# Second chunk's tokens loaded ahead of the third query weights, and the layer-norm statistics of two token tiles moved in the opening of an attention and SwiGLU block

## Chip, cores, metric

One core of one Trainium2 chip (trn2). The metric is the device time of one execution in microseconds (us), lower is better. The kernel before takes 1170.86 us (median of 3 runs, 1169.75 to 1174.22).

A ratio is always the mean time of one kernel's fast runs over the mean of the other's of the same rounds, so it is not quite the ratio of the medians that stand beside it.

## The reference, cut to what matters

```python
def reference(A_x, A_k_cache, A_v_cache, A_wq, A_wo, B_x, B_w_gate, B_w_up, B_w_down, c, w_mod):
    # x: 1 x 2048 x 1024, bf16; 32 query heads of 128, 4 key/value heads, the last 512 keys
    sa, ca, ga, sb, cb, gb = (silu(c) @ w_mod) in six pieces
    h = layernorm(x) * (1 + ca) + sa
    x = x + ga * attention(h, A_k_cache, A_v_cache, A_wq, A_wo)   # q = h @ wq, softmax, @ v, @ wo
    h = layernorm(x) * (1 + cb) + sb
    return x + gb * swiglu(h, B_w_gate, B_w_up, B_w_down)
```

The tokens are worked in four chunks of 512, each of four tiles of 128 tokens. This case is about the first 50 us: chunk 0 (tiles 0 to 3) is normalised and its first query heads are projected, attention over chunk 0 begins, and meanwhile chunk 1 (tiles 4 to 7) has to be loaded, get its mean and reciprocal deviation, be normalised and be transposed by DMA.

## The kernel before

The kernel is written for raw engines. A small tracker (`T.op`) puts each operation into its engine's queue in program order and adds the waits that its buffers need. On VectorE an operation that waits held those behind it: in the changed kernel below, tile 4's normalisation waited 1.21 us for its reciprocal deviation, until 32.65 us, and tile 5's statistics, whose tokens had landed at 28.57, started after it, at 33.11.

The loads, all in the queue of SyncE:

```python
            # ... loads of chunk 0, modulation weights, query weights 0 and 1, k(0)
            for k2 in range(DT // 2):
                load_wsa(k2)
            load_v(0)
            load_k(1)
            load_wq(2)        # query weights of heads 8 to 11, 1 MB
            load_x(1)         # tokens of chunk 1 (tiles 4 to 7), 1 MB
            for gk in range(2, Hkv):
                load_k(gk)
            # ...
```

Statistics, normalisation and transposition of a tile of chunk 1 (`stats` is BN_STATS on half a tile, `aggr` combines the halves on VectorE and makes the reciprocal deviation on GpSimd):

```python
            def ln_stats(t):
                stats(t, t % 2, 0)
                yield
                stats(t, t % 2, 1)
                aggr(t % 8, t % 2)
                yield

            def norm_turn(ch, tt):
                t = ch * TPC + tt
                norm(t, t % 8, t % 2, half=True)                   # VectorE
                T.op(Q_ln[t % 2], lambda: SP.dma_start_transpose(hT[ch % 2][:, :, tt * P:(tt + 1) * P], nscf[t % 2]),
                     reads=[B_ns4[t % 2]], writes=B_hT[ch % 2])
```

The end of the opening:

```python
            q_bias_mm(0, 2, BB)
            q_shifted(0)
            qproj_mm(7, QB0[7], HK, DT)
            q_raw(7)                    # evacuates head 7's bank, on ScalarE
            q_shifted(1)
            for dt in range(DT):
                shift(dt)               # 8 operations on VectorE
            stats_now(TPC)              # tile 4, VectorE
            stats_now(TPC + 1)          # tile 5, VectorE
```

And what each iteration of the attention loop does first. Iteration 1 emits the first scores and the bias matmuls of heads 2 and 3, whose results VectorE copies out of bank `QB` (the "bq copy"); iteration 2 projects head 8 into the same bank, so that projection waits for the bq copy:

```python
            def pre0(i):
                if 2 <= i < NQ0:
                    q_shifted(i)
                # ... the k transposes of iterations 2, 3, 4 and their evacuation on VectorE
                if i == 1:
                    scores(0)
                if i in (1, 3, 5):
                    q_bias_mm(i + 1, i + 3, QB)                    # ends with the bq copy on VectorE
                if i < NQ0 + 1:
                    if i % 2 == 0:
                        qproj(NQ0 - 1 + i // 2)                    # i = 2: head 8, into bank QB
                elif i + 3 < NDI:
                    qproj(i + 3)
                if i < 5:
                    norm_turn(1, i - 1)
                if 1 < i < 4:
                    stats_now(TPC + i)                             # tiles 6 and 7
                # ... modulation of chunk 1 at i = 7 and 8
            # then in the same iteration: scores(i - 1), pv(i - 2)
```

`scores(i)` are 4 matmuls and two exponentials on ScalarE; `pv(i)` multiplies the probabilities with v, and VectorE evicts the product with a reciprocal and a multiplication.

The softmax here doesn't subtract the row's maximum and nothing guards it: scores larger than these inputs give would overflow.

## Time and profile before

| | before |
|---|---|
| median, range (3 runs) | 1170.86 us, 1169.75 to 1174.22 |
| span of the profiled execution | 1168.8 us |
| TensorE busy | 1150.6 us (98%) |
| longest wait of TensorE | 4.18 us, at 31.3 us |

First the page's busy times, engine by engine (us, share of the span, instructions):

```profile
span 1168.8 us, 18210 instructions
PE 1150.6 (98%) x7087; PEld 585.7 (50%) x7087; DVE 819.9 (70%) x1641; ACT 527.6 (45%) x735; POOL 67.3 (6%) x135
```

TensorE has 18 us of idle time in all. Next, the waits of TensorE between 25 and 60 us (who waited for whom; us in total, times, longest):

```profile
PE ps L272 <- DVE bq L668: 4.2, 1, 4.2
PE ps L272 <- ACT arena L790: 0.2, 1, 0.2
PE ps L272 <- DVE arena L812: 0.2, 1, 0.2
```

The timeline shows what stands behind that one wait. Columns: start, duration, engine, line, operation, output and input, count, and in brackets the idle time before it and what ended it:

```profile
29.61 0.60 ACT L658 ACTIVATE arena<-ps 128x512 f32<-128x512 f32 x1 [4.46 <-PE ps L272]
29.89 2.19 DVE L678 TENSOR_SCALAR arena<-arena,mod_bf 128x512 f16<-128x512 f16 x8
30.91 0.38 PE L276 MATMUL ps<-arena 128*128 128x128 bf16 x4
32.10 1.42 DVE L413 BATCH_NORM_STATS2 st<-x_res 128x6 f32<-128x512 bf16 x2
33.56 0.21 DVE L417 BATCH_NORM_AGGREGATE mv<-st 128x2 f32<-128x12 f32 x1
33.69 1.37 DVE L413 BATCH_NORM_STATS2 st<-x_res 128x6 f32<-128x512 bf16 x2
35.09 0.21 DVE L417 BATCH_NORM_AGGREGATE mv<-st 128x2 f32<-128x12 f32 x1
35.22 0.10 DVE L668 COPY bq<-ps 128x2 f32<-128x2 f32 x1
35.47 5.34 PE L272 MATMUL ps<-arena 128*128 128x512 f16 x28 [4.18 <-DVE bq L668]
...
36.57 0.15 PEld L272 LDWEIGHTS ps<-arena 128*128 128x128 bf16 x1 [0.28 <-issue]
36.99 0.15 PEld L272 LDWEIGHTS ps<-arena 128*128 128x128 bf16 x1 [0.28 <-issue]
...
38.94 0.69 DVE L647 CAST arena<-ps 128x512 bf16<-128x512 f32 x1 [2.44 <-PE ps L272]
...
41.74 0.69 DVE L812 TENSOR_TENSOR arena<-ps,rl 128x512 f16<-128x512 f32 x1
42.49 0.68 PE L272 MATMUL ps<-arena 128*128 128x129 bf16 x9 [0.18 <-DVE arena L812]
```

Read it from the top. TensorE is done at 31.29 (30.91 + 0.38). VectorE does the 8 shifts, the statistics of tiles 4 and 5 (L413, L417) and only then the tiny bq copy (L668), which lets head 8's projection start at 35.47. Its weight loads are then 0.42 us apart, against 0.22 us at 22.5 to 24.6 us: the clock is at half rate (granted 0.50 from 35.65 to 39.06 us). VectorE in its turn waits 2.44 us for that slow projection (L647). The last two lines are the first PV eviction and the second PV product, which waits for it. **The start of the second PV product, 42.49 us here, is the point by which I compare all kernels below.**

The chain of waits, followed back from the end of the program, tells the same stretch differently:

```profile
19.50 12.58 DMA x_res<-in_A_x_dram
32.10 0.71 DVE st L413
```

It says that the statistics waited for the landing of chunk 1's tokens, 12.58 us after their issue. But the shifts (29.89 + 2.19) also end at 32.08. The two tie, and the chain names one of them.

### The profile page before, as it was taken

Reading aid. Unit: us, or ns where it says so; the run is one execution under the profiler, and the core shown is the slowest. Engines: PE = TensorE matmul, PEld = TensorE weight load, DVE = VectorE, ACT = ScalarE, POOL = GpSimd, SP = SyncE. Lnnn points to the kernel's source line nnn. Section 1 sums busy time; section 2 is a strip of 40 time slices with the busy share of each in tenths; the row PEclk is TensorE's granted clock in tenths of the full one; section 3 lists DMA queues with packets and bytes.
Section 4 is the critical chain, followed back from the end, with each engine's and each line's share of the span. In section 5 each row is a group of like instructions: output and inputs, shape, how many; then the busy total and the mean of one; then the engine's idle time right before and its main releaser. Section 6 shows DMA issues by size and latency. Waiting matters only on the chain.

```text
span 1168.8 us, 18210 instructions
## 1 busy us (share of the span) xinstructions
PE 1150.6 (98%) x7087; PEld 585.7 (50%) x7087; DVE 819.9 (70%) x1641; ACT 527.6 (45%) x735; POOL 67.3 (6%) x135
## 2 busy tenths in 40 slices
PE   9899999999999999999999999999999999999998
PEld 5465555654445666665444444444444444444443
DVE  4867897748476777777566798767558777776535
ACT  3666777740117777787110345454110444445010
POOL 1100131000000111111000010000000000000000
PEclk9999999999999999999999999999999999999999
DMA  9679899787816888844776232333775424234343
GB/s 325 135 194 213 200 225 211 178 179 203 256 36 161 192 203 187 210 106 107 192 182 187 73 108 73 97 84 99 207 182 156 122 73 109 73 100 133 125 156 108
DMA packets 289765, 179.98 MB, mean 154 GB/s; under 512 B 130448, under 2 KB 277904, under 8 KB 289680
## 3 DMA queue, kind: packets, MB, share of 16 engines
q1 hardware_dynamic: 226736, 92.31, 36.3%
q10 hardware_dynamic: 54304, 55.05, 14.9%
q0 software_dynamic: 8640, 31.46, 9.2%
q8 instruction: 56, 0.92, 0.4%
q14 instruction: 29, 0.24, 0.1%
HBM read 128.45 MB, written 19.92 MB: 127 GB/s over the span
## 4 chain that ended last, share of the span: by engine, by line
PE 90%; DMA 4%; DVE 3%; SPq 2%; issue 1%; ACT 1%; POOL 0%; ACTq 0%; DVEq 0%; POOLq 0%
PE ps L272 90%; DMA arena<-arena 1%; DMA x_res<-in_A_x_dram 1%; DMA wo_sum<-arena 1%; DMA arena<-in_A_wo_dram 1%; DVE arena L820 1%; DVE st L413 1%; DVE arena L891 0%; SPq L382 0%; SPq L341 0%; ACT arena L790 0%; DVE arena L812 0%; SPq L364 0%; SPq L355 0%; ACT nsc L823 0%
## 5 line engine op out<-in xcount | busy, mean ns | idle before, releaser
L272 PE MATMUL ps<-arena 128*128 128x512 f16 (+2 forms) x6782 | 1143.9, 331 | 14.6 <-DVE bq L668 4.2
L272 PEld LDWEIGHTS ps<-arena 128*128 128x128 bf16 (+1 forms) x6782 | 575.6, 98 | 574.9 <-issue 10.0
L790 ACT ACTIVATE arena<-ps 128x1024 bf16<-128x1024 f32 x256 | 261.3, 1022 | 54.8 <-PE ps L272 42.9
L823 ACT ACTIVATE tmp<-ps 128x512 f32<-128x512 f32 x166 | 99.1, 597 | 302.3 <-PE ps L272 289.6
L891 DVE TENSOR_TENSOR arena<-arena 128x512 f16<-128x512 bf16 x328 | 133.1, 418 | 3.1
L820 DVE TENSOR_TENSOR arena<-ps,tmp 128x512 bf16<-128x512 f32 (+1 forms) x134 | 91.8, 685 | 46.1 <-PE ps L272 34.4
L812 DVE TENSOR_TENSOR arena<-ps,rl 128x512 f16<-128x512 f32 x128 | 88.5, 691 | 6.5 <-DMA arena<-arena 2.1
L823 ACT ACTIVATE nsc<-ps 128x512 f32<-128x512 f32 x84 | 50.1, 596 | 93.2 <-PE ps L272 90.9
L820 DVE TENSOR_TENSOR arena<-ps,nsc 128x512 f16<-128x512 f32 x84 | 57.3, 686 | 40.3 <-PE ps L272 31.1
L809 DVE RECIPROCAL rl<-ps 128x4 f32<-128x4 f32 x128 | 23.0, 180 | 87.9 <-PE ps L272 86.8
L1029 DVE TENSOR_TENSOR arena<-arena 128x2048 f16<-128x2048 f16 (+3 forms) x56 | 56.0, 1010 | 13.5 <-PE ps L272 12.9
L1502 ACT ACTIVATE arena<-arena 128x512 f16<-128x512 f16 x84 | 49.9, 624 | 30.7 <-DVE arena L820 30.7
L820 DVE TENSOR_TENSOR tmp<-ps,tmp 128x512 f32<-128x512 f32 x32 | 22.1, 689 | 55.7 <-ACT tmp L823 47.6
L823 ACT ACTIVATE arena<-ps 128x512 f32<-128x512 f32 x16 | 9.6, 598 | 91.9 <-PE ps L272 91.9
L941 DVE TENSOR_TENSOR arena<-arena 128x512 f16<-128x512 bf16 x120 | 47.8, 419 | 2.8 <-DMA arena<-in_A_wo_dram 1.7
L413 DVE BATCH_NORM_STATS2 st<-x_res 128x6 f32<-128x512 bf16 x62 | 42.3, 682 | 4.1 <-DMA x_res<-in_A_x_dram 3.7
L1517 DVE TENSOR_TENSOR arena<-arena 128x512 f16<-128x512 f16 x84 | 34.9, 415 | 0.2
L1097 DVE TENSOR_TENSOR tmp<-tmp,rowb 128x512 f32<-128x512 f32 x48 | 33.2, 692 | 1.6
L427 DVE TENSOR_SCALAR nsc<-x_res,mv,rstd 128x1024 f16<-128x1024 bf16 (+1 forms) x30 | 16.1, 538 | 25.6 <-DMA arena<-nsc 25.6
L594 DVE SCALAR_TENSOR_TENSOR arena<-arena 128x1024 bf16<-128x1024 bf16 x24 | 29.2, 1215 | 0.0
L1098 DVE TENSOR_TENSOR arena<-tmp,x_res 128x512 bf16<-128x512 f32 x32 | 22.1, 692 | 1.1
L820 DVE TENSOR_TENSOR arena<-ps,rowb 128x512 f16<-128x512 f32 x28 | 19.3, 689 | 3.9 <-ACT rowb L823 3.9
(81 smaller groups left out, 326.9 us busy)
## 6 DMA issues: line engine op xcount, KB each, us to landing
arena<-in_A_wq_dram SPq DMA_DIRECT2D x28, 512.0 KB, 5.0
arena<-wo_sum ACTq DMA_DIRECT2D x7, 2048.0 KB, 9.1
arena<-in_B_w_gate_dram SPq DMA_DIRECT2D x28, 512.0 KB, 4.0
arena<-in_B_w_up_dram SPq DMA_DIRECT2D x28, 512.0 KB, 5.0
arena<-wd_sum ACTq DMA_DIRECT2D x8, 1792.0 KB, 8.0
arena<-in_B_w_down_dram ACTq DMA_DIRECT2D x6, 1792.0 KB, 7.3
arena<-in_A_wo_dram POOLq DMA_DIRECT2D x16, 512.0 KB, 5.1
wo_sum<-arena POOLq DMA_DIRECT2D x16, 512.0 KB, 4.9
```

What stands on the lines that cost most here:

```text
L272: T.op(PE, lambda: TE.matmul(out_ap, lhsT, rhs, start=start, stop=stop, skip_group_check=skip), reads=reads, writes=[bank_buf])
L413: T.op(DVE, lambda: V.bn_stats(st_[sl][:, hf * 6:hf * 6 + 6], x_res[:, t, hf * 512:hf * 512 + 512]), reads=[B_x[t]], writes=[B_st[sl]])
L790: T.op(ACT, lambda: A.activation(ex_s[es][:, 2 * kp:2 * kp + 2, :], banks2(SCB + 2 * kp), AF.Exp, scale=att_scale), writes=[PB[SCB + 2 * k ...
L812: T.op(DVE, lambda: V.tensor_tensor(o_s[os_].rearrange("p (a b) d -> p a b d", a=2), psap(PVB * 512, [[512, 2], [130, 2], [1, P]]), rlb, A ...
L820: T.op(DVE, lambda: V.tensor_tensor(out, bank(ba), other, ADD), reads=[ob2], writes=[PB[ba], ob])
L823: T.op(ACT, lambda: A.activation(dst, bank(bk), AF.Copy), writes=[PB[bk], db])
L891: T.op(st, lambda: eng.tensor_tensor(o, a, b, op), reads=rd, writes=[wr])
L941: T.op(DVE, lambda: V.tensor_tensor(o, a, b, SUB), reads=rd, writes=[wr])
L1029: T.op(DVE, lambda: V.tensor_tensor(o, a, b, SUB), reads=rd, writes=[sb])
L1097: T.op(DVE, lambda: V.tensor_tensor(tm, tm, rw, MULT), reads=[B_row[row]], writes=[tb])
L1502: T.op(ACT, lambda: A.activation(o, s_, AF.Silu), reads=[sb], writes=[ob])
L1517: T.op(DVE, lambda: V.tensor_tensor(gu[blk][:, p, :], o, s_, MULT), reads=[sb, ob], writes=[B_gu[blk][p]])
```

## The change

The intent: let the tokens land before the weights; compute the first of the four tiles' statistics on ScalarE, which is idle there, by two passes with an accumulator (sum, then sum of squared differences); and move tile 5's behind the bq copy, into iteration 1, so that tiles 5, 6 and 7 come one per iteration (6 and 7 stay where they were).

```diff
             load_v(0)
             load_k(1)
+            load_x(1)
             load_wq(2)
-            load_x(1)
@@
+            def stats_act(t):
+                sl = t % 8
+                o, ob = nsc4[t % 2], B_ns4[t % 2]
+                T.op(ACT, lambda: A.activation(o, x_res[:, t, :], AF.Copy, accum_out=acc[:, 0:1]), reads=[B_x[t]], writes=[ob, B_acc])
+                T.op(POOL, lambda: g.tensor_scalar(mv[sl][:, 0:1], acc[:, 0:1], 1.0 / D, None, op0=ALU.mult),
+                     reads=[B_acc], writes=[B_mv[sl]])
+                T.op(ACT, lambda: A.activation(o, x_res[:, t, :], AF.Square, bias=mv[sl][:, 0:1], scale=-1.0, accum_out=acc[:, 1:2]),
+                     reads=[B_x[t], B_mv[sl]], writes=[ob, B_acc])
+                rstd_of(sl, acc[:, 1:2], B_acc, 1.0 / D)
@@
             qproj_mm(7, QB0[7], HK, DT)
+            stats_act(TPC)
             q_raw(7)
             q_shifted(1)
             for dt in range(DT):
                 shift(dt)
-            stats_now(TPC)
-            stats_now(TPC + 1)
@@
-                if 1 < i < 4:
+                if 1 <= i < 4:
                     stats_now(TPC + i)
```

## The prediction

> **What bounds the kernel.** The page: TensorE is busy 1150.6 of 1168.8 us (98%), so at most 18 us can be won without removing matmuls. The longest wait of TensorE is 4.2 us on the bias copy (DVE bq), in the opening. The timeline shows it: TensorE ends the first scores and the k transpose at 31.29 us and starts the ninth query projection (head 8) at 35.47. That projection reuses the bank which the bq copy on VectorE frees, and VectorE, in order, first does 8 shifts (29.89 to 32.08) and the statistics of tiles 4 and 5 (32.10 to 35.3). Chunk 1's tokens land at 32.08 (issue 19.50 + 12.58 in the chain), just as the shifts end; wq part 2 lands near 29.2 (issue 18.83 + 10.4). After the gap the projection's 8 matmuls take 3.45 us (0.43 each; 1.89 us for 8 at 22.6): TensorE has gone cold. [...]
>
> **What the change does.**
> 1. Tokens and wq part 2 swap landings (1 MB each, 2.9 us apart): tokens ~29.2, weights ~32.1.
> 2. Tile 4's statistics leave VectorE (two BN_STATS and the aggregate, 1.6 us) for ScalarE, idle between 25.2 and 29.6. Costed with the opening's own such pass (copy 1.06, square 1.15, reads, POOL; 3.7 us end to end): 29.2 to ~32.0 on ScalarE, rstd ready ~33.0.
> 3. Tile 5's statistics move behind the bq copy and tile 4's normalisation.
> New costs: the evacuation of head 7 moves from 29.6 to ~32.0, the first exponentials from 30.28 to ~32.6 (done ~34.8 instead of 32.4).
>
> **On the critical path.** VectorE: shifts end 32.08, bq copy ~32.2, so TensorE starts head 8 at ~32.3 (weights 32.1) instead of 35.47; gap ~1 us, no cold clock, projection ~1.8 instead of 3.45 us. That would be nearly 5 us, but VectorE becomes the limit: it waits for rstd of tile 4 to ~33.0, normalises (0.45), does tile 5's statistics (1.6), shift, k copy, head 8's copy (from ~35.8; before 38.94), normalise 5, statistics 6, then the first PV product's eviction at ~38.6 (before 41.74) . TensorE waits at the second PV (~39.3; before 42.49), of the order of 1 us. VectorE's own sum: 1.6 us of statistics gone, 2.4 us of waiting for the cold projection gone, 0.9 us of new waiting: **3.1 us**. By 47 us everything is about 3.1 us earlier; from there TensorE is saturated, loads are issued from program order and shift along, and I expect the gain kept to the end.
>
> **Predicted: 1170.86 - 3.1 = 1167.8 us, range 1165.3 to 1170.3.** Chances: faster by over 2% 0.01, within 2% 0.98, slower 0.01.
>
> **What would show it.** TensorE's wait on bq of 4.2 us gone, replaced by ~1 us at 31.3 and by 1 to 2 us in waits on ScalarE's exponentials and VectorE's PV eviction before 45 us; head 8's matmuls 0.22 us each; tokens landing ~29.2 and weights ~32.1; ScalarE's two statistics passes 29.2 to 32; the 128x4 reciprocals of the first PV at ~38.5 instead of 41.6; TensorE busy ~1.6 us less in total.
>
> **What would make it wrong.** If loads don't complete in issue order, tokens land later and ScalarE, stuck in order, holds head 7's evacuation and the exponentials: the gain shrinks by the delay. If weights land after ~34, TensorE waits there again. If a later limit that doesn't shift (background weight sums through memory, 159 to 181 us in the chain) takes the 3 us back, the total is unchanged.

## The result

| | before | after |
|---|---|---|
| first comparison, 4 runs each | 1170.88 us (1169.75 to 1174.22) | 1166.36 us (1165.51 to 1167.93) |
| ratio after / before | | 0.9958, 95% interval 0.9935 to 0.9981 |
| span of the profiled execution | 1168.8 us | 1164.3 us |
| all later control runs | 1169.86 us median of 42 | 1166.43 us median of 16 (with the 4 above) |

So the change is 0.3 to 0.4% faster: 4.5 us in the first four runs, 3.4 us over all runs.

The page and the waits of TensorE between 25 and 60 us, after:

```profile
span 1164.3 us, 18217 instructions
PE 1148.6 (99%) x7087; PEld 585.3 (50%) x7087; DVE 818.1 (70%) x1638; ACT 529.4 (45%) x739; POOL 68.9 (6%) x136
```

```profile
PE ps L272 <- DVE arena L821: 1.4, 1, 1.4
PE ps L272 <- DMA arena<-in_A_wq_dram: 1.0, 1, 1.0
PE ps L272 <- ACT arena L799: 0.5, 2, 0.3
```

The wait on the bq copy is gone. In its place are 1.0 us for the weights, 0.5 us for exponentials and 1.4 us for the first PV eviction (L821 is L812 of before). The timeline of the same stretch:

```profile
28.59 1.06 ACT L730 ACTIVATE nsc<-x_res 128x1024 bf16<-128x1024 bf16 x1 [4.14 <-DMA x_res<-in_A_x_dram]
29.19 2.19 DVE L678 TENSOR_SCALAR arena<-arena,mod_bf 128x512 f16<-128x512 f16 x8
30.21 0.38 PE L276 MATMUL ps<-arena 128*128 128x128 bf16 x4
30.39 1.15 ACT L733 ACTIVATE nsc<-x_res,mv 128x1024 bf16<-128x1024 bf16 x1 [0.65 <-POOL mv L731]
31.29 0.15 DVE L668 COPY bq<-ps 128x2 f32<-128x2 f32 x1
31.54 0.58 ACT L658 ACTIVATE arena<-ps 128x512 f32<-128x512 f32 x1
31.62 2.33 PE L272 MATMUL ps<-arena 128*128 128x512 f16 x10 [1.02 <-DMA arena<-in_A_wq_dram]
32.02 4.16 ACT L799 ACTIVATE arena<-ps 128x1024 bf16<-128x1024 f32 x4
32.65 0.55 DVE L427 TENSOR_SCALAR nsc<-x_res,mv,rstd 128x1024 f16<-128x1024 bf16 x1 [1.21 <-POOL rstd L527]
33.11 1.42 DVE L413 BATCH_NORM_STATS2 st<-x_res 128x6 f32<-128x512 bf16 x2
...
35.37 0.68 DVE L647 CAST arena<-ps 128x512 bf16<-128x512 f32 x1
...
38.16 0.69 DVE L821 TENSOR_TENSOR arena<-ps,rl 128x512 f16<-128x512 f32 x1
...
38.91 1.08 PE L272 MATMUL ps<-arena 128*128 128x129 bf16 x16 [1.36 <-DVE arena L821]
```

The tokens land at 28.57 and ScalarE takes tile 4 (L730, L733); the bq copy follows the shifts at once (31.29); head 8 starts when the weights land (31.57); VectorE waits 1.21 us for tile 4's reciprocal deviation and is then the busy engine up to the first PV eviction. The second PV product starts at 38.91.

Lining up the two traces matmul by matmul (both have 7087, in the same order) gives the lead of the changed kernel over the course of the program:

```
where                                   start before   lead of after
200th matmul, before anything changed     24.49          0.70 us
head 8, first matmul                      35.47          3.86
head 8, last matmul                       38.27          5.14
second PV product                         42.49          3.59
up to 70 us                                              3.59
after the waits at 104 to 119 us         118.8           3.85
after a wait at 183 us                   184.0           4.51
end                                                      4.54
```

Of the 4.54 us, 0.70 were there before the change could act, 2.89 came between the opening and the second PV product, and 0.95 came from later waits. By the last matmul of head 8 the change had won 4.44 us (5.14 - 0.70), and 1.55 of them were given back before the second PV product.

### The profile page after: what moved, and what is told of

The parts are those of the page before. It is cut to its first block, busy times and chain, and to the rows that moved or that the text cites. A ratio compares the mean times of both kernels' runs of the same rounds, so it can differ in the third digit from the quotient of the medians.

```text
span 1164.3 us, 18217 instructions
## 1 busy us (share of the span) xinstructions
PE 1148.6 (99%) x7087; PEld 585.3 (50%) x7087; DVE 818.1 (70%) x1638; ACT 529.4 (45%) x739; POOL 68.9 (6%) x136
## 4 chain that ended last, share of the span: by engine, by line
PE 91%; DVE 3%; DMA 3%; SPq 1%; ACT 1%; issue 1%; POOL 0%; DVEq 0%; ACTq 0%; POOLq 0%
PE ps L272 91%; DMA arena<-arena 1%; DMA x_res<-in_A_x_dram 1%; DVE arena L829 1%; DMA arena<-in_A_wo_dram 1%; DVE st L413 1%; SPq L382 0%; DVE arena L900 0%; DMA wo_sum<-arena 0%; SPq L341 0%; ACT arena L799 0%; SPq L364 0%; DVE arena L821 0%; ACT nsc L832 0%; SPq L310 0%
## 5 line engine op out<-in xcount | busy, mean ns | idle before, releaser
L821 DVE TENSOR_TENSOR arena<-ps,rl 128x512 f16<-128x512 f32 x128 | 88.5, 691 | 6.0 <-DMA arena<-arena 1.6
```

The costliest lines, as they stand in the source:

```text
L821: T.op(DVE, lambda: V.tensor_tensor(o_s[os_].rearrange("p (a b) d -> p a b d", a=2), psap(PVB * 512, [[512, 2], [130, 2], [1, P]]), rlb, A ...
```

## Experiments

Theory: (1) VectorE's order of work, not the landing of the tokens, held TensorE; (2) behind that, VectorE's chain from the shifts to the first PV eviction is the limit, so what counts is when that chain starts and how much stands in it; (3) the clock at half rate is part of the cost of the gap. The main rivals: the tokens' landing was the limit (the chain of waits), or all that counts is TensorE's own wait.

For each run I give the time and, from its one profile, the lead of the second PV product over the before profile, with the lead at 24.5 us (most of it comes from the clock at the very start, see the end of "The clock alone") taken off. I call it the net lead.

| run | median us (runs) | ratio to before, 95% interval | net lead at the second PV |
|---|---|---|---|
| the change, first comparison | 1166.36 (4) | 0.9958, 0.9935 to 0.9981 | 3.59 - 0.70 = 2.89 |
| e0_change_again | 1166.52 (6) | 0.9965, 0.9945 to 0.9985 | 3.23 - 0.36 = 2.87 |
| e10_change_control | 1166.79 (6) | 0.9972, 0.9958 to 0.9987 | 3.02 - 0.54 = 2.48 |
| e1_loads_only | 1171.55 (6) | 1.0007, 0.9992 to 1.0021 | -0.07 - 0.40 = -0.47 |
| e2_old_loads | 1168.70 (6) | 0.9991, 0.9978 to 1.0004 | 0.15 - 0.16 = -0.01 |
| e3_order_only | 1168.68 (6) | 0.9986, 0.9973 to 0.9999 | 0.42 - 0.23 = 0.19 |
| e4_warm | 1167.32 (6) | 0.9976, 0.9964 to 0.9988 | 1.56 - 0.57 = 0.99 |
| e5_tile4_dve | 1169.15 (6) | 0.9991, 0.9968 to 1.0013 | 2.05 - 0.60 = 1.45 |
| e6_tokens_earlier | 1165.04 (6) | 0.9953, 0.9936 to 0.9971 | 3.27 + 0.09 = 3.36 |
| e7_stats_later | 1166.76 (6) | 0.9967, 0.9949 to 0.9985 | 3.37 + 0.51 = 3.88 |
| e8_combined | 1167.24 (5) | 0.9967, 0.9953 to 0.9981 | 4.85 + 0.04 = 4.89 |
| e9_order_warm | 1168.98 (5) | 0.9988, 0.9972 to 1.0004 | 1.19 - 0.27 = 0.92 |
| e11_tokens_earlier_warm | 1165.03 (5) | 0.9969, 0.9955 to 0.9982 | 3.91 - 0.52 = 3.39 |

All gave the right result. The intervals of the ratios reach 1.4 to 2.7 us to each side, so the times alone separate only the larger differences; the net lead separates finer ones, but it is one execution each.

### The loads alone

```diff
+            load_x(1)
             load_wq(2)
-            load_x(1)
```

> The kernel before with only the two loads swapped. My theory (VectorE's program order is what held TensorE: shifts end at 32.08 us and the statistics of tiles 4 and 5 stand ahead of the bias copy): tokens land near 28.6 to 29.2, but VectorE still reaches the statistics only at about 32.1, so TensorE's wait on the bias copy stays 3.9 to 4.3 us and the total within 0.5 us of before. Rival (the profile's chain names the landing of the tokens, 12.6 us, so their landing was the limit): VectorE's statistics start up to 3 us earlier, the wait shrinks to about 1 us, and the total falls by about 3 us.

Measured: ratio 1.0007. The tokens landed at 29.21 us, nearly 3 us sooner, and VectorE took no notice. Its timeline, from the shifts to head 8:

```profile
29.48 2.19 DVE L678 TENSOR_SCALAR arena<-arena,mod_bf 128x512 f16<-128x512 f16 x8
31.59 1.42 DVE L413 BATCH_NORM_STATS2 st<-x_res 128x6 f32<-128x512 bf16 x2
...
34.94 6.29 PE L272 MATMUL ps<-arena 128*128 128x512 f16 x28 [4.05 <-DVE bq L668]
```

The statistics still start when the shifts end, and TensorE still waits 4.05 us. The rival that the tokens' landing was the limit is ruled out, although the chain of waits had named it. VectorE kept its program order here: the data were in place 2.4 us early (29.21 against 31.59 us), and the statistics did not move past the shifts.

Also worth a look: the group of 28 matmuls took 6.29 us here against 5.34 before. I come back to that.

### All but the loads

Against the changed kernel:

```diff
-            load_x(1)
             load_wq(2)
+            load_x(1)
```

> The changed kernel with the loads in the old order. My theory: the swap matters only together with ScalarE's pass. Tokens land near 32, the ScalarE pass takes 4.0 us to the reciprocal deviation, so normalisation of tile 4 starts at about 36 us (32.65 after the change), head 7's evacuation at about 35, and although TensorE starts head 8 at about 32.3 without a cold clock, the second PV starts at about 42.4 us as before the change (42.49): total 0 to 0.7 us faster than before. Rival (the gain is TensorE's own wait on the bias copy plus the cold clock, 3 to 5 us at head 8): at least 3 us faster than before.

Measured: net lead -0.01 us as expected, 1168.70 us. The tokens landed at 32.30, TensorE started head 8 at 32.13 (lead 3.3 us) and ran it at full rate (lead 4.6 us at its last matmul), then waited 2.5 us for the first exponentials, which stood behind ScalarE's statistics, and 1.4 us for the first PV eviction. Three lines of its timeline, those between left out:

```profile
32.13 1.89 PE L272 MATMUL ps<-arena 128*128 128x512 f16 x8 [0.99 <-DVE bq L668]
36.08 0.55 DVE L427 TENSOR_SCALAR nsc<-x_res,mv,rstd 128x1024 f16<-128x1024 bf16 x1 [4.09 <-POOL rstd L527]
42.34 1.08 PE L272 MATMUL ps<-arena 128*128 128x129 bf16 x16 [1.37 <-DVE arena L821]
```

VectorE waited 4.09 us for tile 4's reciprocal deviation, so its chain started late and its first PV eviction came no sooner than before. So 4.5 us won at head 8 (4.63 - 0.16) were worth nothing at the second PV product. The rival that TensorE's own wait is all that counts falls. The total was 1 us lower (1 - 0.9991, of 1170), a little more than the 0 to 0.7 us that I had expected, and not clear of zero.

Loads and ScalarE's pass are therefore one change: the first is worth nothing alone (e1), the rest nearly nothing without it (e2).

### The order alone, and with a warm clock

Only tile 5's statistics moved behind the bq copy, everything else as before:

```diff
             stats_now(TPC)
-            stats_now(TPC + 1)
@@
-                if 1 < i < 4:
+                if 1 <= i < 4:
```

> The kernel before, with only tile 5's statistics moved into iteration 1 (loads old, tile 4 on VectorE as before). My theory: bias copy at about 33.7, TensorE waits about 2.5 us instead of 4.2, [...]head 8 ready before VectorE wants it, normalisation of tile 4 near 34.6 after its reciprocal deviation, second PV about 1.6 us earlier than before; total about 1.6 us faster. Rival (ScalarE's pass and the swap carry the gain): under 0.5 us.

Measured: net lead 0.19, not 1.6; the time 1.6 us lower (ratio 0.9986, barely clear of 1). I had put the gap at 2.5 us and counted with no half rate; it was 3.1 us, and the clock did go cold: the trace's clock record has half rate from 33.3 to 40.1 us, 6.8 us, twice as long as in the before profile. The same kernel with dummy matmuls in that gap:

```diff
+                if i == 2:
+                    warm(12, PVB + 1)      # 12 matmuls into a bank that is free then
                 if i < NQ0 + 1:
                     if i % 2 == 0:
                         qproj(NQ0 - 1 + i // 2)
```

> The run with the order alone changed (tile 5's statistics in iteration 1), plus 12 dummy matmuls before head 8. That run fell short of its 1.6 us at the second PV (0.2), and its clock record shows 6.8 us at half rate from 33.3 us. My theory: the cold clock is the cause. With the dummies the clock stays up, the lead at the second PV, less that at 24 us, is 1.3 to 1.7 us, and the mean granted clock is 1.0 in all runs. Rival (the chain of VectorE is longer than I think): the lead stays under 0.6 us with a warm clock.

Measured: no half rate in its profile, net lead 0.92: between the two theories. Another 0.5 us is visible: with the old loads the tokens landed only at about 32.3, and VectorE waited 0.5 us for them. The times do not separate the two runs (1168.68 and 1168.98), and two of the five runs still had a mean clock below 1. That the clock cost e3 its gain is supported by its profile and not shown by its time.

### The clock alone

The kernel before with 18 dummy matmuls in the 4.2 us gap, nothing else changed:

```diff
+                if i == 2:
+                    warm(18, PVB + 1)
```

> The kernel before plus 18 dummy matmuls into a free bank in the gap before head 8 (nothing else changed; the result stays right). It measures the cold clock by itself. My theory: head 8's 8 matmuls take about 1.9 us instead of 3.45, VectorE's wait of 2.4 us for that projection shrinks by 1.6 us, the second PV starts about 1.6 us earlier and the total is about 1.6 us lower. Rival (the cold clock cost nothing, VectorE was the limit anyway): under 0.4 us.

Measured: 1167.32 us, ratio 0.9976, 2.8 us less: **dummy work in a gap that stays where it is brings more than half of what the change brings** (3.3 to 4.9 us by the ratios); the interval of e4's own ratio is 1.4 to 4.2 us. The timeline shows head 8 starting at the same time as before, and the group of 28 matmuls taking 3.66 us instead of 5.34:

```profile
35.46 3.66 PE L272 MATMUL ps<-arena 128*128 128x512 f16 x28 [0.84 <-DVE bq L668]
...
37.38 0.69 DVE L647 CAST arena<-ps 128x512 bf16<-128x512 f32 x1 [0.89 <-PE ps L272]
```

VectorE's wait for the projection fell from 2.44 to 0.89 us, the 1.6 us that I had expected. The second PV product started 1.56 us earlier (net 0.99: the opening was 0.57 ahead in this execution, but the tokens landed no sooner and VectorE waited 0.59 us for them). The total fell by more than that. Two things can have added to it, and no run separates them. In the two profiles the lead grows from 1.55 us at 107 us to 3.6 at the end, since this execution had none of the later waits of the before profile, which come and go (see "The change again"). And most runs of the kernel before lose more to the clock than its profile shows. Every run has a mean granted clock (1.0 is full rate throughout, apart from the warm-up at the start, which it does not count: in the before profile the 128x512 matmuls followed each other 0.43 us apart from 3.7 to 8.3 us and 0.22 us apart from 8.8 us on, and the windows show 1.00 for both):

```
mean clock        1.0     0.998-0.999    0.997    0.996     (runs)
before, 42 runs     0         8            29        5      medians 1169.04 / 1170.16 / 1170.35
the change, 16     10         5             1        0      medians 1166.34 / 1167.70 / 1170.33
e4_warm, 6          6         0             0        0
```

In the profiles, 0.998 and 0.999 go with one stretch of 3.41 us at half rate, and 0.997 with two of them (6.83 us, in e1 and e3). By these figures, an estimate, 34 of 42 runs of the kernel before lose two stretches or more, and the one that I had the profile of (0.999) is by its clock among the better ones, though not by its time (1170.72 us). In the six profiles that have half rate the stretches lie on a grid of steps of 3.41 us: in the before profile full rate began at 8.34 us, half rate at 35.65, which is 8 times 3.413 later, and ended at 39.06; in the five others it began 8, 10 or 11 such steps after full rate did. In the before profile the gap puts 1.0 us of idle time into one step of the grid and 3.2 us into the next, and one stretch followed; in e1 it puts in 2.6 and 1.4 us, and two followed. So in these two profiles it went with where the grid lay whether much the same gap cost one stretch or two. Windows of three profiles show it, the columns being start and end, width, busy time of TensorE, weight loads, VectorE, ScalarE and GpSimd, then the granted clock, the DMA share and GB/s. Before:

```profile
32.00:36.00 4.00, 0.53 (x2) 0.28 (x3) 3.83 (x10) 0.42 (x1) 1.32 (x4) 0.96 0.14 32
36.00:40.00 4.00, 4.00 (x16) 1.58 (x15) 1.56 (x4) 0.49 (x1) 0.60 (x1) 0.62 0.35 66
```

e1, where all that differs is the loads:

```profile
32.00:36.00 4.00, 1.06 (x3) 0.44 (x4) 3.85 (x10) 0.01 (x1) 1.85 (x4) 0.69 0.12 27
36.00:40.00 4.00, 4.00 (x10) 1.37 (x9) 1.45 (x3) 0.59 (x1) 0.07 (x1) 0.50 0.35 66
```

The changed kernel (first profile):

```profile
32.00:36.00 4.00, 3.73 (x32) 2.03 (x29) 3.28 (x8) 3.82 (x5) 1.46 (x3) 1.00 0.40 78
36.00:40.00 4.00, 2.53 (x40) 1.81 (x41) 3.90 (x11) 2.22 (x3) 1.03 (x2) 1.00 0.62 72
```

The third column from the end is the granted clock. With 0.50 over the whole of 36 to 40 us, e1 got 9 weight loads done where before got 15 (the changed kernel is further on by then and has other matmuls). That is where e1's 6.29 us come from, and its lead falls from 0.39 us at head 8's last matmul to -0.27 within this stretch. The clock record accounts for both without the loads.

The warm-up differs from profile to profile: full rate was first reached between 5.8 and 8.3 us. This also explains most of the lead at 24.5 us. At about 8 us the change's lead is 0.90 us, half of the 1.81 us by which its full rate began sooner (6.53 us against 8.34). Part of such a lead is lost again before 24.5 us, in e6, e7 and e8 by 0.4 to 0.6 us at 20.3 to 20.8 us, where TensorE waits for query weights.

### Tile 4 back on VectorE, behind the bq copy

```diff
-            stats_act(TPC)
@@
+                if i == 1:
+                    stats_now(TPC)
                 if i < 5:
                     norm_turn(1, i - 1)
```

> The changed kernel with tile 4's statistics back on VectorE, but behind the bias copy (in iteration 1, before its normalisation). TensorE's wait before head 8 is then as short as in the change (about 1 us, no cold clock). My theory (VectorE's chain to the first PV's eviction is the limit): normalisation of tile 4 about 1.3 us later (34.0 instead of 32.65), second PV about 40.2 instead of 38.9, total 1.0 to 1.5 us above the changed kernel. Rival (freeing the bias copy is all that mattered): same as the changed kernel within 0.4 us.

Measured: net lead 1.45, that is 1.44 less than the change, as expected from VectorE's chain; normalisation of tile 4 at 34.18, 1.5 us later than in the change (two lines of the timeline):

```profile
34.18 0.55 DVE L427 TENSOR_SCALAR nsc<-x_res,mv,rstd 128x1024 f16<-128x1024 bf16 x1 [1.07 <-POOL rstd L420]
40.44 1.91 PE L272 MATMUL ps<-arena 128*128 128x129 bf16 x16 [1.36 <-DVE arena L820]
```

TensorE's gap before head 8 was 1.4 us here (the weights landed at 32.08), close to the changed kernel's, so the chain theory holds and "freeing the bq copy is all" falls. The total is 2.6 us above the control (1169.15 against 1166.52), more than expected; the profile shows one more stretch at half rate, from 40.3 to 43.7 us, after two gaps of 1.34 and 1.36 us. It took another 1.5 us of lead (2.05 at the second PV product, 0.54 at 58 us).

### The change again

> The changed kernel once more, as the control of this call and for a second profile of it. My theory: of the 4.5 us between the two profiles 2.9 belong to the opening (head 8 to the second PV) and come back in any execution of the change; 0.7 came from when the clock warmed up at the very start and about 0.95 from two waits at 107 to 118 and 183 us on DMA landings, and those vary from execution to execution. So lead over the before profile at the second PV, less the lead at 24 us, 2.9 within 0.3; no cold clock in the opening; total 3 to 4.5 us under before. If the later 0.95 us belongs to the change, waits of TensorE on the PV eviction between 60 and 200 us stay at 0.5 or less here.

Measured: net lead 2.87 against 2.89, no half rate, 1166.52 us. The lead of the opening comes back exactly. The later part does not: here the waits at 104 to 119 us cost this execution 1.8 us (lead 3.23 at 70 us, 1.22 at 112 us, 2.28 at 119 us), and the end lead was 3.25 instead of 4.54. The gaps of TensorE over 0.6 us between 60 and 230 us, in all profiles but e11's (which lacks 86 of its 7091 matmul records):

```
before 0.97          the change none / 1.83 / 1.84    e1 1.30, 0.75     e2 none
e3 1.68              e4 none                       e5 0.69           e6, e7, e8 none      e9 0.66
```

They come and go without regard to the kernel. Two of them (before, and the change's 1.84) are waits for a PV eviction whose output buffer is still being transposed by DMA. In three (the change's 1.83, e1's 1.30, e3's) the PV eviction stood behind an operation of VectorE that waited 2.4 to 2.9 us for output weights to land. The three small ones (0.66 to 0.75) waited for an eviction behind other work of VectorE. Between 102 and 115 us such a transposition took 7 to 13 us to land in the before profile, against 2.4 to 4 us in a quiet stretch, while tokens, query weights and output weights were being loaded. That DMA traffic is the cause is what the landings suggest; no run removed it.

### Less waiting in VectorE's chain

Tokens still earlier (in front of v(0) and k(1), with v(0) behind the weights):

```diff
-            load_v(0)
-            load_k(1)
             load_x(1)
+            load_k(1)
             load_wq(2)
+            load_v(0)
```

> The changed kernel with chunk 1's tokens moved further ahead, in front of the first v and the second k slice, and the v slice behind wq part 2. My theory: tokens land about 0.7 us earlier (27.9), tile 4's reciprocal deviation comes 0.7 us earlier, VectorE's wait for it falls from 1.2 to about 0.5, the second PV starts at about 38.2; total 0.5 to 0.8 us under the changed kernel. Rival (that wait is hidden elsewhere): no difference at the second PV.

Measured: net lead 3.36, 0.5 us more than the change; VectorE waited 0.73 us before tile 4's normalisation instead of 1.21. 1165.04 us against the control's 1166.52, five of six runs below the lowest of 16 runs of the change (1165.51). The net lead rests on taking off what e6 lost at 20.4 us, where its own order of loads may have had a part; without that it would be 2.9 us, as in the change. But e11 below, with the same order and no such wait, has 3.39. So 0.5 us of it is explained; the rest may be that at most one of its six runs had a stretch at half rate.

Tile 6's and 7's statistics one place later, so that they don't stand ahead of the first PV eviction:

```diff
-                if i < 5:
-                    norm_turn(1, i - 1)
-                if 1 <= i < 4:
-                    stats_now(TPC + i)
+                if i in (1, 2, 4, 5):
+                    norm_turn(1, {1: 0, 2: 1, 4: 2, 5: 3}[i])
+                if i in (1, 3, 4):
+                    stats_now(TPC + {1: 1, 3: 2, 4: 3}[i])
```

> The changed kernel with tile 6's and 7's statistics and normalisations one place later in VectorE's order, so that tile 6's statistics no longer stand in front of the first PV's eviction. My theory: TensorE's wait of 1.4 us on that eviction goes, second PV at about 37.5 instead of 38.9, total 1.0 to 1.4 us under the changed kernel. It could be taken back where tile 7's transposition lands one iteration later (modulation at about 51 us). Rival (TensorE is bound by the exponentials there): under 0.4 us.

Measured: net lead 3.88, 1.0 us more than the change: TensorE's 1.4 us wait on the first PV eviction was indeed VectorE's queue. But the total was that of the control (1166.76, 1166.52), so my expectation for it failed: by 70 us the lead had fallen from 3.66 to 1.51. Tile 7 came late, as feared: VectorE's waits between 44 and 70 us have a line that the changed kernel doesn't have:

```profile
DVE arena L432 <- DMA arena<-nsc: 1.3, 1, 1.3
```

That is the modulation of chunk 1 waiting for tile 7's transposition, which landed at 54.21 us. But matmul by matmul the lead fell by 0.2 us at 44.8, 1.1 at 46.4, 0.5 at 56.5 and 0.3 at 57.7, so only the last 0.8 us can come from that landing. The largest step is the old wait moved one iteration on: TensorE waited for a PV eviction that now stood behind tile 7's statistics.

```profile
43.90 1.41 DVE L413 BATCH_NORM_STATS2 st<-x_res 128x6 f32<-128x512 bf16 x2
46.38 5.23 PE L272 MATMUL ps<-arena 128*128 128x129 bf16 x50 [0.95 <-DVE arena L821]
```

Both together, with tile 7's statistics on ScalarE and its normalisation in time:

```diff
+            def tick0(i):
+                if i == 3:
+                    stats_act(TPC + 3, tmp[1].bitcast(BF16)[:, :], B_tmp[1])
+                if i == 4:
+                    norm_turn(1, 3)
```

(on top of e6, with `norm_turn` at i = 1, 2, 4 for tiles 4, 5, 6 and `stats_now` at i = 1, 3 for tiles 5, 6)

> The run with earlier tokens, and in addition VectorE's chain relieved: tile 6's statistics behind the first PV's eviction (as in the run before, where that took TensorE's wait there away), tile 7's statistics on ScalarE in its idle stretch after the third pair of exponentials, tile 7's normalisation at the end of the fourth iteration so that its transposition is not late again. My theory: lead at the second PV, less the lead at 24 us, about 4.3 us (2.9 in the change), kept at 70 us this time (2.0 in the run that put tile 7 late); total 1 to 2 us under the changed kernel and about 5 us under before. If tile 7 is late again (VectorE waiting for the transposition at the modulation near 51 us), the gain is taken back as before.

Measured: net lead 4.89, the best of all, and tile 7 in time; yet 1167.24 us, no better than the control's 1166.79. My expectation for the total failed. ScalarE's second pair of passes held the next exponentials, TensorE had two new gaps (0.89 us before 43.7, 0.51 before 44.8), and at 45.16 a stretch of 3.41 us at half rate began. Lead, by the time of the before profile: 5.1 at 47 us, 1.44 at 58 us.

### The control, with a cold stretch

> The changed kernel as the control of this call. Lead at the second PV, less the lead at 24 us, 2.9 us as in its two other profiles; median 1166 to 1167; most runs with a mean granted clock of 1.0; gaps of TensorE at 100 to 120 us between 0 and 1.8 us, differing from its other profiles.

Measured: 1166.79 us, but a net lead of 2.48, and this profile of the change does have half rate (33.1 to 36.5 us):

```profile
32.00:36.00 4.00, 3.32 (x9) 1.23 (x10) 2.82 (x7) 2.47 (x4) 1.40 (x4) 0.64 0.43 88
```

The weights landed at 32.63 here, and the gap before head 8 was 1.93 us. So here a gap of 1.93 us was followed by a stretch. It cost only 0.4 us of net lead, because it used up slack: the waits that the first profile has after head 8, 0.5 us for exponentials and 1.4 us for the first PV eviction, are 0.2 us and none here. In this execution TensorE itself was the limit up to the second PV product.

### Dummies in the remaining gap

e6 with 4 dummy matmuls (`warm(4, PVB + 1)`) ahead of head 8, where the third profile of the change had its gap of 1.93 us and then half rate.

> The run with earlier tokens plus 4 dummy matmuls (about 0.9 us) in TensorE's remaining gap before head 8, which is about 1.0 us long. [...] My theory: [...]no execution falls below a mean clock of 0.999, the lead at the second PV less that at 24 us stays at about 3.3 us, and the time is 1164.5 to 1165.7 us median, 4 to 5 us under before, at or just under the run with earlier tokens. If the gap before the second PV (1.4 us) is what drops the clock, some runs still show 0.998 to 0.999 and the median is no better than 1165.0.

Measured: mean clock 1.0 in all five runs, net lead 3.39, median 1165.03 (1164.89 to 1168.07). So it is level with e6 by the median and not better; its ratio to the before runs, 0.9969, is no better than the change's (0.9958 to 0.9972). e6 and e11 are about 1.4 us (0.1%) under the changed kernel by their medians. I would take e6; whether the dummies add anything is open.

## Why the prediction was right

The prediction was 1167.8 us (1165.3 to 1170.3), and the result 1166.36, inside the range. Point by point:

1. **"VectorE, in order", not the loads, held TensorE: right.** e1 moved the tokens by 2.9 us and changed nothing.
2. **Loads: right.** Predicted tokens 29.2 and weights 32.1; measured 28.57 and 31.57, with the opening 0.7 us early. The risk named, completion out of issue order, did not occur: in every profile here the two 1 MB loads landed in the order of their issue (before: weights 29.2 and tokens 32.08; after: tokens 28.57 and weights 31.57).
3. **ScalarE's pass: right but for 0.3 us.** Predicted 3.7 us end to end; from the landing at 28.57 to the reciprocal deviation at 32.56 it took 4.0, the mean on GpSimd taking 0.53 where the opening's own took 0.24. VectorE waited 1.21 instead of 0.9 us. The passes themselves took 1.06 and 1.15 us.
4. **Gap, clock and given-back gain: right.** Predicted: gap of 1 us, no cold clock, nearly 5 us at head 8, then VectorE as the limit and 1 to 2 us of new waits, first PV's reciprocal at 38.5. Measured: 1.02 us, no cold clock in the first two profiles (the third has one), 4.44 us, waits of 1.36 and 0.5 us, 37.99. TensorE's busy time fell by 2.0 us, where 1.6 was predicted. e2 (all of the gain at head 8 lost) and e5 (1.44 us less for 1.5 us more in the chain) show that the limit was VectorE's chain, not only argue it.
5. **The sum of 3.1 us: measured 2.89 and 2.87** at the second PV in two profiles, 2.48 in a third.
6. **Kept to the end: right.** The lead of the first profile was 3.59 from 42 to 107 us. What varies later varies without the change.

The total agrees partly by luck. Of the 4.54 us between the first two profiles 1.65 belong to the start and to the later waits, and the 1170.86 us that I started from is 1.0 us above the median of the 42 later runs. With a range of 2.5 us to each side the total says little; what confirms the mechanism is the 2.9 us at the second PV product.

One term of the sum may have been mis-sized: "2.4 us of waiting for the cold projection gone". It was read from one profile, and that execution had lost one stretch of 3.41 us at half rate, where by the mean clock 34 of 42 runs lose at least two. Runs of the kernel before with 0.997 are 1.1 us slower by the median than those with 0.999, though the two groups overlap. An estimate from these: 3.1 us + 0.8 x 1.1 us is 4.0 us, from which the stretches that the change's own runs lose (6 of 16 are below 1.0) would have to be taken off. Measured were 3.4 us over all runs and 4.5 us in the first four. That the clock makes up this difference is argued and not shown: the interval of the first comparison, 2.2 to 7.6 us, holds them all. That a gap of about 1 us would bring no cold clock, and in e3 one of about 2.5 us, was assumed: no run had shown it beforehand. e3's gap was 3.1 us, and 6.8 us at half rate followed.

Three things stay open: how much of e3's missing gain the clock took, how much of e4's 2.8 us (only 1.0 us is seen at the second PV product), and what decides the size of the waits at 104 to 119 us.

## What to carry to other kernels

When an engine waits for a small operation, look at what stands ahead of that operation in its own engine's queue before blaming the data it reads; moving the data alone (e1) changed nothing, and moving only the queue (e2) changed nearly nothing, because the next queue became the limit. Follow the lead of the change matmul by matmul: a gain at the first wait says little until the next common limit is passed. And price a gap of TensorE with the clock in it (before: a gap of 4.18 us, then 3.41 us at half rate): filling a gap with dummy matmuls that shortened nothing (e4) won 2.8 us where the change wins 3.3 to 4.9, so it is a cheap test and sometimes a cheap fix.

## Further measurements

- Gaps of TensorE shorter than the 4.18 us of the kernel before were followed by stretches at half rate too: one of 1.93 us (the change, third profile) and two of 0.89 and 0.51 us (e8) by one stretch, one of 3.1 us even by two (e3). Other gaps of 1.0 to 1.4 us, and one of 2.49 us (e2), cost none. Nor does the idle time within one step of the grid decide it: 1.40 us (e8) was followed by half rate, 1.70 us (e2) was not.
- The number of stretches differs from run to run: by their mean clock, 8 of 42 runs of one kernel lost one, 34 lost two or more, and their medians are about 1.1 us apart.
- Batch-norm operations on VectorE: BN_STATS on 128x512 bf16 took 0.7 us, the aggregation of two of them 0.2 us.
- A 128x1024 two-byte transposition within SBUF (256 KB) landed 3.2 us after its issue in a quiet stretch (the change, tile 4) and 6.4 us among other loads (tile 7).
